# Regrouping the first loads on two hardware queues, whole score stages, and a remade instruction order, in a hashed-attention and feed-forward kernel

## The chip, the cores and the metric

The kernel runs on one core of one Trainium2 chip. The time is device microseconds of one execution; a run's time is 1.7 to 2.8 us (mostly 1.7) longer than the span of its profile, which runs from the first to the last instruction. Before the change the median of 3 runs was 319.82 us (319.4 to 319.95). Differences of a per cent are discussed here, so kernels that are compared ran on the same chip in the same rounds. All ratios are the mean time of one kernel's fast runs over the mean of the other's fast runs of the same rounds, so they are not quite the ratios of the medians quoted beside them.

## The reference

```python
# q, k, v: (4, 8, 768, 64) float32, proj: (64, 6), w_ch1: (512, 2048), w_ch2: (2048, 512)
q_bits = (q @ proj > 0);  k_bits = (k @ proj > 0)            # 6 hash bits for each row
mask   = bucket(q_bits)[..., :, None] == bucket(k_bits)[..., None, :]
scores = where(mask, q @ k.T / 8, -1e9)
attn   = softmax(scores)                                     # row sum + 1e-9
x      = (attn @ v)  -> (4, 768, 512)
xn     = (x - mean) / sqrt(var + 1e-6) * g_ln
out    = x + relu(xn @ w_ch1) @ w_ch2
```

(Shortened.) The attention of a batch feeds a feed-forward block on the same rows.

## The kernel before

The kernel is a list of words, each of which emits one small group of instructions. A word is `name.engine.arguments`; engines are `t` TensorE, `v` VectorE, `a` ScalarE, `p` GpSimd and `s` the queue of SyncE. Every engine executes its own words strictly in the order of the list; only tile dependences join the engines. The whole schedule is thus that list, and changing it is changing the program.

```python
def lx(eng, g, t, kp):              # one third of q (t=0) or k (t=1) of batch 0, head group g: 256 KB
    src = qk_view(t, 0, g).rearrange("p (c kp x) -> p kp c x", c=CC, kp=3)
    dst = Xt(0, g, t).rearrange("p (c kp x) -> p kp c x", c=CC, kp=3)
    eng.dma_start(out=dst[:, kp], in_=src[:, kp])
def lv(eng, b, hs, c):              # V of 4 heads, 32 partitions: 192 KB
    eng.dma_start(out=vnat(b, hs)[32*c:32*c+32], in_=v_view[b][c][:, hs:hs+4])
def tn(eng, g, t, kp): ...          # VectorE: 32x32 transposes of a third of batch 0      X  -> tp
def tu(eng, b, g, t, n): ...        # VectorE: the same for batches 1 to 3                  X  -> T
def ca(...), CA(...): ...           # cast to bf16, on VectorE, ScalarE or GpSimd           tp/T -> qb, kb
def ha(...); def bi(...)            # TensorE hash product hf; VectorE makes its bits G
def cv(...); def su(...)            # GpSimd: V to bf16 (vaug); three additions to vsum
def sp(...); def sc(...)            # TensorE vp <- vsum; copy to vsB (a correction of the row sums)
# ... cut ...
def S_(eng, s, h): ...              # scores of stage s; h=0, 1: two heads each, h=2: all four
def E_(eng, s, h): ...              # ScalarE: exponential of two heads
def A_(eng, s, h): ...              # attention times V, summed in PSUM over 6 stages of a unit
def na, nb, nc_, ce: ...            # VectorE: y; division x <- y,rc; statistics; xc <- x,mv,gB
def fl(eng, u, t): ...              # DMA transpose xnT <- xc (unit 0: TensorE "ft" and a copy "fc")
def F_(eng, u, p): ...              # first layer, f <- xnT,w_sb: 8 matmuls
def R_(eng, u, p): ...              # relu hb <- f, on VectorE or ScalarE
def D_(eng, u, t, qtr): ...         # second layer, f <- w_sb,hb: 4 matmuls
def Z_(...); def O_(...)            # res on VectorE; the output's DMA
```

The work is 12 units of 256 rows, each with 6 score stages. The first layer of unit 0 can start only when stages 0 to 5 have been multiplied with V, divided and normalised; from then on the matmuls of one unit fill the gaps of the next one's attention.

The softmax here doesn't subtract the row's maximum and nothing guards it: scores larger than these inputs give would overflow.

Of the kernel before, what the change touches and what calls it, by code (L numbers as in the profile page):

```python
# [17 lines left out]
mem.v lp.a pf.v lx.s.0.1.1 warm.t tn.v.0.1.1 lx.s.0.0.0 tn.v.0.0.0 ca.a.0.0.0 ha.t.0.0.0 lx.s.0.1.0 tn.v.0.1.0  # L18
pmem.p lx.s.1.0.0 lx.s.0.0.1 lx.s.0.1.2 bi.v.0.0.0 lx.s.1.1.1 lx.s.1.1.0 p32.p lv.s.0.0.0 lv.s.0.0.1 ha.t.0.1.0
bi.v.0.1.0 lv.s.0.0.2 lv.s.0.0.3 on.p.0 ha.t.0.1.1 ca.a.0.1.0 S.t.0.0 S.t.0.1 E.a.0.0 lx.s.1.1.2 bi.v.0.1.1 E.a.0.1  # L20
ca.p.0.1.1 tn.v.0.1.2 ha.t.0.1.2 tn.v.1.0.0 tn.v.1.1.0 S.t.1.0 ca.v.1.0.0 S.t.1.1 E.a.1.1 ca.v.0.1.2 tn.v.1.1.1
ha.t.1.1.0 E.a.1.0 lv.s.0.4.3 lx.s.1.0.1 bi.v.0.1.2 ha.t.1.1.1 bi.v.1.1.1 S.t.2.1 E.a.2.1 S.t.2.0 lv.s.0.4.0
ca.p.1.1.1 ca.v.1.1.0 ha.t.1.0.0 bi.v.1.0.0 cv.p.0.0.0 cv.p.0.0.2 A.t.1.1 A.t.2.1 A.t.0.1 su.p.0.0 A.t.0.0 E.a.2.0
A.t.2.0 S.t.4.0 E.a.4.0 S.t.4.1 E.a.4.1 lv.s.0.4.1 tn.v.1.0.1 tn.v.0.0.1 ha.t.0.0.1 A.t.1.0 tn.v.1.1.2 ca.p.1.1.2
lg.s lx.s.1.0.2 ca.v.0.0.1 bi.v.1.1.0 sp.t.0.0 sc.v.0.0 S.t.3.0 ha.t.1.1.2 E.a.3.0 na.v.0.0 nb.v.0.0 S.t.3.1 E.a.3.1
bi.v.1.1.2 S.t.5.0 ha.t.1.0.1 E.a.5.0 S.t.5.1 bi.v.0.0.1 S.t.6.0 ca.v.1.0.1 tn.v.1.0.2 ca.v.1.0.2 lw1.p.2 lx.s.0.0.2
tn.v.0.0.2 ca.v.0.0.2 lv.s.0.4.2 cv.p.0.4.2 A.t.4.1 cv.p.0.4.0 A.t.4.0 A.t.3.0 A.t.5.0 nc.v.0.0 bi.v.1.0.1 A.t.3.1
on.p.1 E.a.5.1 S.t.7.1 A.t.5.1 su.p.0.4 sp.t.0.4 sc.v.0.4 na.v.0.1 nb.v.0.1 lw1.p.1 lw1.p.0 E.a.6.0 S.t.8.0 E.a.7.1
S.t.6.1 A.t.6.0 lw1.p.3 E.a.8.0 S.t.9.0 A.t.8.0 lv.s.1.4.1 lw2.p.2 E.a.6.1 A.t.6.1 E.a.9.0 S.t.8.1 E.a.8.1 S.t.7.0
E.a.7.0 S.t.9.1 E.a.9.1 A.t.7.1 A.t.8.1 lw2.p.1 lw2.p.0 A.t.7.0 lv.s.1.4.0 LX.s.1.0.0 tu.v.1.0.0.3 tu.v.1.0.0.0  # L30
tu.v.1.0.0.1 tu.v.1.0.0.2 nc.v.0.1 ce.v.0.1 ft.t.0.1 fc.a.0.1 ce.v.0.0 rs.p.0 ft.t.0.0 S.t.11.2 E.a.11.1 E.a.11.0
lw2.p.3 LX.s.1.0.1 tu.v.1.0.1.0 tu.v.1.0.1.1 tu.v.1.0.1.3 lv.s.1.4.2 fc.v.0.0 F.t.0.5 F.t.0.4 R.v.0.5 F.t.0.3
R.v.0.4 R.a.0.3 S.t.10.2 E.a.10.0 F.t.0.2 R.a.0.2 tu.v.1.0.1.2 CA.p.1.0.1 na.v.1.0 A.t.9.0 A.t.11.2 nb.v.1.0
nc.v.1.0 A.t.9.1 ha.t.0.0.2 bi.v.0.0.2 E.a.10.1 A.t.10.2 na.v.1.1 nb.v.1.1 nc.v.1.1 ce.v.1.0 fl.s.1.0 ce.v.1.1
fl.s.1.1 F.t.0.0 R.a.0.0 F.t.0.1 R.a.0.1 S.t.14.2 E.a.14.0 E.a.14.1 hm.t.1.0 bt.v.1.0 mo.s.1.0.0.2 mo.s.1.0.1.2
mo.s.1.0.2.1 mo.s.1.0.0.3 F.t.0.7 R.a.0.7 F.t.0.6 R.a.0.6 A.t.14.2 S.t.13.2 E.a.13.0 LX.s.1.1.0 mo.s.1.0.3.2
D.t.0.0.0 D.t.0.0.1 D.t.0.0.2 E.a.13.1 A.t.13.2 S.t.12.2 E.a.12.1 F.t.1.0 R.a.1.0 mo.s.1.0.1.3 D.t.0.0.3 Z.v.0.0
F.t.1.7 mo.s.1.0.3.3 CA.p.1.0.0 tu.v.1.1.0.0 tu.v.1.1.0.3 ha.t.1.0.2 bi.v.1.0.2 LX.s.1.1.1 tu.v.1.1.1.0 tu.v.1.1.1.2
tu.v.1.1.1.3 lv.s.1.0.1 rs.p.1 lv.s.1.4.3 su.p.1.4 E.a.12.0 tu.v.1.1.0.1 mo.s.1.0.0.1 mo.s.1.0.1.0 mo.s.1.0.2.3
mo.s.1.0.1.1 mo.s.1.0.3.1 R.a.1.7 F.t.1.5 R.a.1.5 S.t.16.2 E.a.16.0 tu.v.1.1.1.1 mo.s.1.0.2.2 A.t.12.2 E.a.16.1  # L40
lv.s.1.0.2 mo.s.1.0.2.0 mo.s.1.0.3.0 lv.s.1.0.3 F.t.1.4 R.a.1.4 lv.s.1.0.0 cv.p.1.0.2 cv.p.1.4.0 D.t.0.1.0 S.t.17.2
E.a.17.0 E.a.17.1 mo.s.1.0.0.0 tu.v.1.1.0.2 CA.v.1.1.0 hm.t.1.1 bt.v.1.1 mo.s.1.1.2.1 mo.s.1.1.3.3 mo.s.1.1.0.0
mo.s.1.1.0.2 mo.s.1.1.1.1 D.t.0.1.1 mo.s.1.1.3.0 cv.p.1.0.0 sp.t.1.4 sc.a.1.4 mo.s.1.1.2.3 S.t.15.2 E.a.15.0
E.a.15.1 na.v.2.0 A.t.17.2 A.t.16.2 nb.v.2.0 nc.v.2.0 mo.s.1.1.1.3 F.t.1.1 D.t.0.1.2 mo.s.1.1.3.1 tab.a R.v.1.1
mo.s.1.1.3.2 A.t.15.2 na.v.2.1 nb.v.2.1 nc.v.2.1 ce.v.2.1 ce.v.2.0 rs.p.2 fl.s.2.1 fl.s.2.0 F.t.1.2 R.a.1.2
mo.s.1.1.0.1 S.t.18.2 E.a.18.0 E.a.18.1 CA.v.1.1.1 D.t.0.1.3 Z.v.0.1 mo.s.1.1.1.2 F.t.1.3 R.a.1.3 mo.s.1.1.1.0
S.t.20.2 E.a.20.1 E.a.20.0 F.t.1.6 A.t.18.2 su.p.1.0 D.t.1.0.0 D.t.1.0.1 D.t.1.0.2 R.v.1.6 sp.t.1.0 sc.a.1.0
S.t.19.2 E.a.19.1 E.a.19.0 F.t.2.0 R.v.2.0 D.t.1.0.3 Z.v.1.0 mo.s.1.1.2.2 mo.s.1.1.0.3 F.t.2.2 R.v.2.2 on.p.2
mo.s.1.1.2.0 S.t.22.2 E.a.22.0 E.a.22.1 A.t.20.2 F.t.2.7 R.v.2.7 D.t.1.1.0 S.t.21.2 E.a.21.0 E.a.21.1 LX.s.2.0.0
tu.v.2.0.0.0 D.t.1.1.1 LX.s.2.0.1 tu.v.2.0.1.0 tu.v.2.0.1.2 LX.s.2.1.0 F.t.2.4 O.s.0.2 R.a.2.4 tu.v.2.0.0.3 O.s.0.0  # L50
A.t.19.2 na.v.3.0 nb.v.3.0 LX.s.2.1.1 S.t.23.2 E.a.23.1 F.t.2.1 R.v.2.1 O.s.0.3 nc.v.3.0 cv.p.1.4.2 lv.s.2.4.0
lv.s.2.4.2 lv.s.2.0.3 lv.s.2.0.1 lv.s.2.0.2 lv.s.2.4.3 A.t.22.2 lv.s.2.4.1 A.t.21.2 tu.v.2.0.1.3 F.t.2.3 R.v.2.3
E.a.23.0 A.t.23.2 na.v.3.1 nb.v.3.1 nc.v.3.1 ce.v.3.0 fl.s.3.0 S.t.25.2 E.a.25.0 E.a.25.1 F.t.2.5 R.a.2.5
tu.v.2.0.1.1 D.t.1.1.2 D.t.1.1.3 S.t.24.2 E.a.24.0 E.a.24.1 F.t.2.6 R.a.2.6 A.t.25.2 Z.v.1.1 O.s.1.0 D.t.2.0.0
O.s.1.2 O.s.1.3 ce.v.3.1 fl.s.3.1 CA.v.2.0.1 tu.v.2.0.0.1 S.t.26.2 E.a.26.0 E.a.26.1 D.t.2.0.1 O.s.0.1 tu.v.2.0.0.2
LX.s.3.0.1 hm.t.2.0 bt.v.2.0 mo.s.2.0.1.0 mo.s.2.0.0.3 mo.s.2.0.2.1 mo.s.2.0.3.1 mo.s.2.0.0.0 mo.s.2.0.1.2
mo.s.2.0.2.0 mo.s.2.0.0.1 mo.s.2.0.3.2 S.t.28.2 E.a.28.0 E.a.28.1 F.t.3.2 R.v.3.2 su.p.2.4 A.t.26.2 A.t.24.2
na.v.4.0 nb.v.4.0 F.t.3.4 R.v.3.4 CA.p.2.0.0 tu.v.2.1.1.3 tu.v.2.1.0.0 tu.v.2.1.0.1 S.t.27.2 E.a.27.1 E.a.27.0
tu.v.2.1.0.3 mo.s.2.0.0.2 LX.s.3.1.1 D.t.2.0.2 D.t.2.0.3 Z.v.2.0 F.t.3.3 R.a.3.3 tu.v.2.1.1.2 A.t.27.2 S.t.29.2
E.a.29.1 cv.p.2.4.0 nc.v.4.0 F.t.3.0 R.v.3.0 A.t.28.2 D.t.2.1.0 mo.s.2.0.1.1 F.t.3.1 R.v.3.1 lv.s.2.0.0 cv.p.2.0.0  # L60
cv.p.2.0.2 mo.s.2.0.1.3 O.s.1.1 mo.s.2.0.3.0 E.a.29.0 A.t.29.2 S.t.30.2 E.a.30.0 E.a.30.1 na.v.4.1 nb.v.4.1 F.t.3.7
R.a.3.7 D.t.2.1.1 D.t.2.1.2 S.t.32.2 E.a.32.1 mo.s.2.0.2.2 F.t.3.5 A.t.30.2 nc.v.4.1 ce.v.4.1 fl.s.4.1 ce.v.4.0
fl.s.4.0 R.v.3.5 D.t.2.1.3 Z.v.2.1 O.s.2.2 O.s.2.0 su.p.2.0 F.t.3.6 R.v.3.6 E.a.32.0 A.t.32.2 mo.s.2.0.3.3
tu.v.2.1.1.1 S.t.31.2 E.a.31.0 E.a.31.1 tu.v.2.1.0.2 CA.p.2.1.0 LX.s.3.0.0 F.t.4.5 R.v.4.5 D.t.3.0.0 mo.s.2.0.2.3
F.t.4.6 R.v.4.6 rs.p.4 S.t.33.2 E.a.33.0 O.s.2.3 O.s.2.1 D.t.3.0.1 tu.v.2.1.1.0 CA.p.2.1.1 LX.s.3.1.0 hm.t.2.1
bt.v.2.1 mo.s.2.1.2.3 mo.s.2.1.0.2 mo.s.2.1.2.0 mo.s.2.1.3.2 mo.s.2.1.2.1 tu.v.3.0.1.3 mo.s.2.1.3.1 mo.s.2.1.2.2
mo.s.2.1.3.0 mo.s.2.1.0.1 mo.s.2.1.1.3 mo.s.2.1.1.2 mo.s.2.1.0.0 E.a.33.1 S.t.34.2 E.a.34.0 E.a.34.1 F.t.4.0 R.v.4.0
tu.v.3.0.0.0 D.t.3.0.2 D.t.3.0.3 sp.t.2.0 sc.a.2.0 rs.p.3 A.t.31.2 na.v.5.0 Z.v.3.0 S.t.35.2 E.a.35.0 E.a.35.1
F.t.4.3 R.v.4.3 tu.v.3.0.1.0 A.t.33.2 mo.s.2.1.1.1 A.t.34.2 nb.v.5.0 nc.v.5.0 tu.v.3.0.0.3 F.t.4.2 R.a.4.2 A.t.35.2
na.v.5.1 on.p.3 S.t.37.2 E.a.37.0 E.a.37.1 F.t.4.7 R.a.4.7 mo.s.2.1.1.0 D.t.3.1.0 D.t.3.1.1 S.t.36.2 E.a.36.1  # L70
E.a.36.0 D.t.3.1.2 D.t.3.1.3 F.t.4.1 R.a.4.1 tu.v.3.0.1.2 nb.v.5.1 S.t.38.2 E.a.38.0 nc.v.5.1 ce.v.5.1 fl.s.5.1
ce.v.5.0 rs.p.5 fl.s.5.0 A.t.37.2 F.t.4.4 R.a.4.4 mo.s.2.1.0.3 mo.s.2.1.3.3 Z.v.3.1 O.s.3.0 O.s.3.3 O.s.3.1
D.t.4.0.0 D.t.4.0.1 tu.v.3.0.1.1 CA.p.3.0.1 F.t.5.3 R.v.5.3 A.t.36.2 E.a.38.1 S.t.39.2 E.a.39.1 E.a.39.0 F.t.5.4
R.v.5.4 D.t.4.0.2 D.t.4.0.3 Z.v.4.0 S.t.40.2 E.a.40.0 E.a.40.1 tu.v.3.0.0.2 F.t.5.0 R.v.5.0 A.t.38.2 na.v.6.0
nb.v.6.0 D.t.4.1.0 sp.t.2.4 sc.a.2.4 O.s.3.2 S.t.41.2 E.a.41.0 E.a.41.1 F.t.5.6 cv.p.2.4.2 A.t.40.2 lv.s.3.4.1
A.t.39.2 lv.s.3.4.2 lv.s.3.4.3 R.v.5.6 F.t.5.7 R.a.5.7 S.t.42.2 E.a.42.1 E.a.42.0 A.t.41.2 F.t.5.1 R.a.5.1
lv.s.3.0.1 D.t.4.1.1 D.t.4.1.2 lv.s.3.0.0 nc.v.6.0 S.t.44.2 E.a.44.0 F.t.5.2 R.a.5.2 D.t.4.1.3 na.v.6.1 A.t.42.2
# [41 lines left out]
def kernel(  # L119
# [15 lines left out]
    nc = tc.nc  # L135
# [13 lines left out]
    A = 4 * (D + 1)  # L149
# [139 lines left out]
    def lx(eng, g, t, kp):  # L289
        src = qk_view(t, 0, g).rearrange("p (c kp x) -> p kp c x", c=CC, kp=3)  # L290
        dst = Xt(0, g, t).rearrange("p (c kp x) -> p kp c x", c=CC, kp=3)
        eng.dma_start(out=dst[:, kp], in_=src[:, kp])  # L292
# [254 lines left out]
```

## Time and profile before

| | profile before | timed |
|---|---|---|
| span or time | 325.0 us (its own run took 326.67) | 319.82 us |
| mean granted clock | 0.957 | |
| first first-layer matmul | 51.65 us | |

The profile that was at hand before the prediction fell in an execution with a longer stretch of half clock. Its lines must not be compared with a fast profile directly; a fast profile of the same kernel was taken later (called "the control" below, span 318.9 us).

From the profile page of the kernel before: the slices (40 equal ones, busy tenths), the granted TensorE clock, the DMA share, and what was moved.

```profile
span 325.0 us, 9793 instructions
...
PE   6869999999989999999999999999999999999993
...
PEclk9995558999999999999999999999999999999999
DMA  7999799146117981463154140111220400402122
GB/s 198 216 219 275 130 205 162 23 133 165 51 38 272 302 189 57 144 173 119 22 146 86 32 117 0 39 25 23 53 53 2 114 20 2 99 2 48 50 67 65
```

TensorE looks full after the first five slices. The three 5s in the clock are the slow stretch (24 to 51 us). The DMA engines are busy from the second slice to the seventh, at 130 to 275 GB/s, 201 in the mean. The table of windows of the kernel before says of the later part (columns: the window, its length, busy us and instruction count of each engine, clock, DMA share, GB/s):

```profile
200.00:300.00 100.00, 100.00 (x1474) 67.68 (x1472) 54.71 (x105) 61.41 (x69) 14.44 (x17) 1.00 0.17 38
```

TensorE has no idle time there at full clock. Two groups of the kernel before that matter later (line, engine, operation, tiles, shapes, count; busy us and mean ns of one; idle time before and what ended it):

```profile
L487 DVE TENSOR_SCALAR hb<-f 128x512 bf16<-128x512 f32 x53 | 36.6, 691 | 63.8 <-PE f L477 63.5
...
L442 DVE TENSOR_TENSOR x<-y,rc 128x512 f32<-128x512 f32 x24 | 18.4, 767 | 0.8
```

Source line numbers shift by three or four from one version to another; the tile names are what identifies a line.

### The profile page before, as it was taken

The page shows a single profiled execution, that of the slowest core. Times are in us where ns is not written, and L with a number is a line of the kernel's source. Part 1 is how long each engine was busy: PE and PEld are TensorE (multiplying, and loading weights), DVE is VectorE, ACT ScalarE, POOL GpSimd, SP SyncE. Part 2 cuts the span into 40 slices and gives each one's busy share as a digit, 9 for nine tenths or more (in the row PEclk, how much of TensorE's full clock was granted, in tenths as well). Part 3 has the DMA queues.
Part 4 walks back from the last instruction along what each step waited for, and adds up shares of the span by engine and source line. Part 5 has one row for each costly group of instructions (what it writes and reads, how often), then busy time and mean ns, then how long its engine had stood idle before and what let it go on. Part 6 is the DMA issues. An engine that isn't in the chain of part 4 may idle for free.

```text
span 325.0 us, 9793 instructions
## 1 busy us (share of the span) xinstructions
PE 310.7 (96%) x4320; PEld 211.8 (65%) x4320; DVE 182.9 (56%) x356; ACT 182.0 (56%) x198; POOL 91.5 (28%) x102
## 2 busy tenths in 40 slices
PE   6869999999989999999999999999999999999993
PEld 6555767766656767657677667666667666766651
DVE  4547475716645958765825628914635546446441
ACT  3553476666456676646756656764776675771000
POOL 2065822603470054474220056700300100001000
PEclk9995558999999999999999999999999999999999
DMA  7999799146117981463154140111220400402122
GB/s 198 216 219 275 130 205 162 23 133 165 51 38 272 302 189 57 144 173 119 22 146 86 32 117 0 39 25 23 53 53 2 114 20 2 99 2 48 50 67 65
DMA packets 33354, 33.59 MB, mean 103 GB/s; under 512 B 15648, under 2 KB 29984, under 8 KB 33312
## 3 DMA queue, kind: packets, MB, share of 16 engines
q1 hardware_dynamic: 29008, 28.77, 34.9%
q0 software_dynamic: 4224, 4.19, 8.0%
q8 instruction: 34, 0.56, 0.8%
q14 instruction: 8, 0.07, 0.1%
q10 hardware_dynamic: 80, 0.00, 0.0%
HBM read 27.53 MB, written 6.29 MB: 104 GB/s over the span
## 4 chain that ended last, share of the span: by engine, by line
PE 78%; DMA 8%; DVE 6%; SPq 4%; POOL 2%; issue 1%; ACT 0%; DVEq 0%; ACTq 0%
PE f L477 24%; PE f L492 23%; PE sc L405 17%; PE acc L420 11%; DMA X<-in_q_dram 4%; DMA vn<-in_v_dram 3%; SPq L382 2%; PE hp L370 2%; DVE xc L450 2%; DMA X<-in_k_dram 2%; PE hf L306 2%; SPq L292 1%; DVE st L446 1%; DVE x L442 1%; DVE y L433 1%
## 5 line engine op out<-in xcount | busy, mean ns | idle before, releaser
L411 ACT ACTIVATE E<-sc,bias_sb 128x1024 bf16<-128x1024 f32 x144 | 153.7, 1111 | 82.2 <-PE sc L405 80.3
L477 PE MATMUL f<-xnT,w_sb 128*128 128x256 bf16 x768 | 99.2, 273 | 0.5 <-DVE hb L487 0.5
L492 PE MATMUL f<-w_sb,hb 128*128 128x512 bf16 x384 | 93.6, 379 | 0.0
L477 PEld LDWEIGHTS <-w_sb 128*128 128x128 bf16 x768 | 70.8, 98 | 23.4 <-issue 9.9
L487 DVE TENSOR_SCALAR hb<-f 128x512 bf16<-128x512 f32 x53 | 36.6, 691 | 63.8 <-PE f L477 63.5
L405 PE MATMUL sc<-qb,kb 32*128 32x256 bf16 x1152 | 62.9, 281 | 0.0
L492 PEld LDWEIGHTS <-hb 128*128 128x128 bf16 x384 | 35.6, 98 | 35.4 <-issue 3.8
L405 PE MATMUL sc<-G 6*128 6x256 bf16 x576 | 48.6, 285 | 0.4 <-ACT E L411 0.2
L420 PEld LDWEIGHTS <-E 128*128 128x128 bf16 x1152 | 43.3, 100 | 8.0 <-issue 5.1
L420 PE MATMUL acc<-vaug,E 128*128 128x65 bf16 x1152 | 46.9, 198 | 0.2 <-POOL vaug L328 0.2
L405 PEld LDWEIGHTS <-kb 32*128 32x128 bf16 x1152 | 35.5, 98 | 3.2
L485 ACT ACTIVATE hb<-f 128x512 bf16<-128x512 f32 x43 | 25.6, 596 | 20.6 <-PE f L477 20.5
L455 POOL TENSOR_SCALAR rs<-mv 128x2 f32<-128x2 f32 x12 | 8.5, 710 | 98.1 <-DVE mv L449 97.8
L497 DVE SCALAR_TENSOR_TENSOR res<-f,rs,x 128x512 f32<-128x512 f32 x24 | 17.9, 745 | 28.3 <-PE f L492 21.6
L405 PEld LDWEIGHTS <-G 6*128 6x128 bf16 x576 | 17.3, 94 | 22.4 <-issue 19.5
L244 DVE STREAM_TRANSPOSE T<-X 128x384 f32<-128x384 f32 x48 | 24.9, 553 | 3.6 <-DMA X<-in_k_dram 3.4
L336 POOL TENSOR_TENSOR t<-vn 128x768 f32<-128x768 f32 x8 | 15.2, 1905 | 34.6 <-DMA vn<-in_v_dram 20.2
L328 POOL CAST vaug<-vn 128x768 bf16<-128x768 f32 x16 | 13.9, 889 | 39.0 <-DMA vn<-in_v_dram 30.3
L433 DVE SCALAR_TENSOR_TENSOR y<-vsB,acc 128x520 f32<-128x520 f32 x24 | 16.5, 689 | 9.0 <-PE acc L420 8.7
L450 DVE SCALAR_TENSOR_TENSOR xc<-x,mv,gB 128x512 bf16<-128x512 f32 x24 | 19.9, 829 | 0.9
L306 PE MATMUL hf<-tp,pfull 128*128 128x256 f32 x48 | 15.1, 447 | 5.2 <-DVE tp L244 4.2
L442 DVE TENSOR_TENSOR x<-y,rc 128x512 f32<-128x512 f32 x24 | 18.4, 767 | 0.8
(49 smaller groups left out, 153.1 us busy)
## 6 DMA issues: line engine op xcount, KB each, us to landing
vn<-in_v_dram SPq DMA_DIRECT2D x32, 192.0 KB
out_dram<-res SPq DMA_DIRECT2D x44, 128.0 KB
X<-in_q_dram SPq DMA_DIRECT2D x6, 768.0 KB
X<-in_k_dram SPq DMA_DIRECT2D x6, 768.0 KB
w_sb<-in_moe_w_ch_dram POOLq DMA_DIRECT2D x8, 512.0 KB, 11.1
X<-in_k_dram SPq DMA_DIRECT2D x6, 256.0 KB
X<-in_q_dram SPq DMA_DIRECT2D x6, 256.0 KB
G<-B SPq DMA_DIRECT2D x96, 4.5 KB
```

What stands on the lines that cost most here:

```text
L244: nc.vector.transpose(d[:, j], s[:, j, kj0 : kj0 + n])
L306: nc.tensor.matmul(hf(g, t, kp)[:, :256], pfull[:, j], tp(g, t, kp)[:, j], start=(j == 0), stop=(j == 1))
L405: nc.tensor.matmul(sc(s, i // 2)[:, i % 2, 256 * kk : 256 * kk + 256], lh, rh, start=(rep == 0), stop=(rep == 2), skip_group_check=True,)
L411: nc.scalar.activation(E(s)[:, heads(h)], sc(s, h), AF.Exp, scale=EXP_SCALE, bias=bias_sb)
L420: nc.tensor.matmul(acc[:, qt, (D + 1) * i : (D + 1) * (i + 1)], E(s)[:, i, 256 * kk + P * qt : 256 * kk + P * qt + P], vaug(u // 3)[:, 4 * ...
L433: nc.vector.scalar_tensor_tensor(yt(u, g), vs, EPS_ROW, made[f"acc{u}{g}"][:, :, :A], op0=AOP.mult, op1=AOP.add,)
L442: nc.vector.tensor_tensor(xo, a[:, :, :, 0:D], rc.to_broadcast([P, 2, 4, D]), op=AOP.mult)
L450: nc.vector.scalar_tensor_tensor(xc(u)[:, t], xt(u)[:, t], mv(u)[:, t, 0:1], gB, op0=AOP.subtract, op1=AOP.mult,)
L477: nc.tensor.matmul(f1[:, n].rearrange("p (t x) -> p t x", t=2), w1_sb[:, dt, P * nt : P * nt + P], xnT(u)[:, :, dt], start=(dt == 0), stop ...
L485: nc.scalar.activation(hb(u)[:, 2 * p : 2 * p + 2], f1, AF.Relu)
L487: eng.tensor_scalar_max(hb(u)[:, 2 * p : 2 * p + 2], f1, 0.0)
L492: nc.tensor.matmul(f2, hb(u)[:, nt, P * t : P * t + P], w2_sb[:, nt], start=(nt == 0), stop=(nt == NNT - 1),)
```

## The change

The intent: bring the data of batch 0 in fewer, larger transfers over both hardware queues; emit the scores, and the products with V, of the first ten stages for four heads at once; and let the first layer start after 9 score stages instead of 11. The whole list of words was made anew for this. The code changes little:

```diff
-    def lx(eng, g, t, kp):
-        src = qk_view(t, 0, g).rearrange("p (c kp x) -> p kp c x", c=CC, kp=3)
-        dst = Xt(0, g, t).rearrange("p (c kp x) -> p kp c x", c=CC, kp=3)
-        eng.dma_start(out=dst[:, kp], in_=src[:, kp])
+    def lx(eng, g, t, kp0, kp1):
+        src = qk_view(t, 0, g).rearrange("p (c kp x) -> p c kp x", c=CC, kp=3)
+        dst = Xt(0, g, t).rearrange("p (c kp x) -> p c kp x", c=CC, kp=3)
+        eng.dma_start(out=dst[:, :, kp0:kp1], in_=src[:, :, kp0:kp1])
```

The head of the list (the list has 1,113 words, before 1,138; those that follow are in another order too; cut):

```diff
-mem.v lp.a pf.v lx.s.0.1.1 warm.t tn.v.0.1.1 lx.s.0.0.0 tn.v.0.0.0 ca.a.0.0.0 ha.t.0.0.0 lx.s.0.1.0 tn.v.0.1.0
-pmem.p lx.s.1.0.0 lx.s.0.0.1 lx.s.0.1.2 bi.v.0.0.0 lx.s.1.1.1 lx.s.1.1.0 p32.p lv.s.0.0.0 lv.s.0.0.1 ha.t.0.1.0
-bi.v.0.1.0 lv.s.0.0.2 lv.s.0.0.3 on.p.0 ha.t.0.1.1 ca.a.0.1.0 S.t.0.0 S.t.0.1 E.a.0.0 lx.s.1.1.2 bi.v.0.1.1 E.a.0.1
 ... cut ...
+lx.s.0.1.0.1 on.p.0 mem.v lx.s.0.0.0.1 pmem.p tn.v.0.1.0 warm.t lx.s.0.1.1.3 lx.s.1.0.0.1 lp.a pf.v lv.s.0.4.3
+ca.a.0.1.0 lv.a.0.0.0 lv.s.0.0.3 lv.a.0.4.1 tn.v.0.0.0 ca.a.0.0.0 ha.t.0.1.0 bi.v.0.1.0 lv.a.0.0.1 ha.t.0.0.0
+bi.v.0.0.0 S.t.0.2 E.a.0.1 E.a.0.0 lv.s.0.0.2 tn.v.0.1.1 ha.t.0.1.1 ca.p.0.1.1 tn.v.0.1.2 ca.p.0.1.2 ha.t.0.1.2
+lx.a.0.0.1.3 tn.v.1.0.0 ca.v.1.0.0 cv.p.0.0.2 p32.p bi.v.0.1.1 S.t.1.2 E.a.1.0 bi.v.0.1.2 ha.t.1.0.0 bi.v.1.0.0
+cv.p.0.0.0 A.t.0.2 lw1.p.2 E.a.1.1 S.t.2.2 E.a.2.1 E.a.2.0 lx.s.1.1.0.3 tn.v.1.1.2 ca.p.1.1.2 tn.v.1.1.1 tn.v.1.1.0
+ca.v.1.1.1 ca.v.1.1.0 ha.t.1.1.1 bi.v.1.1.1 ha.t.1.1.0 LX.s.1.0.1 tu.v.1.0.1.0 tu.v.1.0.1.1 tu.v.1.0.1.3
 ... cut ...
```

At the end of the list five output transfers go to ScalarE's queue.

## The prediction

> What bounds it now. By the table of windows, TensorE is busy 199.5 of the 200 us between 100 and 300 at full clock: nothing can be won there. Costing every group at its full-clock step in the chain of waits (relu-layer group of 8 matmuls 0.87 us, second-layer group of 4 0.86, four-head score 0.77, attention-times-V 0.49, hash group about 0.95), all TensorE work comes to about 287 us, 67 of it before 100 us. So some 33 us are lost in the first 100 us of the profiled run (span 325.0). That run had the clock at 0.50 from 24.1 to about 51 us (timeline slices and windows); the timed runs (319.8) are some 7 us shorter, so I take them as mostly unthrottled, with about 26 us lost, nearly all before the first layer of unit 0 starts (51.7 us in the profile, by my estimate 44 to 45 in a timed run). There the limits are: DMA engines saturated from 2 to 32 us at only 180 to 300 GB/s; ScalarE, which needs 2 x 1.11 us of exponentials for each score stage; and TensorE's own order (it waits from 20.8 to 23.2 us for a q transpose that the next scores do not need). The Trainium skill, "TensorE: Matmul & The Clock Gate" (HAM clock gate), says that idle windows halve the clock; the trace agrees: 0.50 just after that gap.
>
> What changes. (1) Scores and products of ten stages go from two halves to whole: two halves took 1.08 us against 0.77, so about 3 us of TensorE, but in a stretch where TensorE is not the limit. (2) Batch-0 q/k loads: 12 issues of 256 KB (0.55 to 0.72 us of queue each) become 7; six loads move to ScalarE's queue. The skill's "DMA: Bandwidth & Descriptors" (Issuing engines are not separate DMA queues) says that both queues share the same 16 engines; the trace, saturated with one queue alone, agrees, so I expect only 1 to 2 us from issue time and longer runs, not a doubled rate. (3) The order: first layer after 9 score stages instead of 11; the q kp1 hash comes after the scores of unit 0; weights are requested from about 14 us on instead of 25 and 35; all V of batch 1 is requested early; V loads still come as 32-partition pieces at about 200 GB/s. The counts of matmuls, exponentials and elementwise work stay.
>
> Estimate. First layer of unit 0 starts at 36 to 37 us, held by the 768 KB k load (about 17 us), then by the batch-1 k load, for whose transposes VectorE waits before the bits of stage 3 (about 24 us), then by 2.2 us of ScalarE per stage. TensorE has then done about 22 us of work; 265 remain, plus 4 to 5 us of switches and a wait for the third weight chunk, plus about 4.8 us of tail and 1.7 us between span and time: about 313. Output issues split over two queues at the end save perhaps 0.5 us.
>
> Prediction: 313 us, 8 in 10 between 306.5 and 318.5. Chances: over 2% faster 0.52, within 2% 0.45, slower 0.03.
>
> Signs. Windows: TensorE saturated from about 40 us on; work after 100 us unchanged at about one lost us in 200. First first-layer matmul at 33 to 40 us. ScalarE exponentials of the first six stages done by about 30 us. DMA share near full until 45 to 50 us, same GB/s for V.
>
> What would make it wrong: a clock at 0.50 in the timed runs of one kernel only (up to 8 us either way); early batch-1 and weight loads delaying the last k load or the first weights (the gain vanishes); or loads much faster than 250 GB/s with longer runs (first layer near 31 us, time near 307).

## The result

| | before, same job | after |
|---|---|---|
| median | 319.88 us (319.4 to 320.76, 4 runs) | 329.13 us (328.3 to 330.21, 4 runs) |
| ratio | | 1.0288, 95% interval 1.0247 to 1.0329 |
| profile | (slow one, above) | span 327.0 us, clock 0.976 |

The kernel became slower by 2.9%, against a predicted gain of 2%; the time lies well outside the range. A second measurement of the same file gave 1.0239 (below). From the profile page of the kernel after, the same lines:

```profile
span 327.0 us, 9752 instructions
...
PE   6737879989979989999999999799999999899994
...
PEclk9769799999999999999999999999999999999998
DMA  6999999311289737120129014121210210402222
GB/s 173 172 272 241 213 304 280 59 36 28 85 149 288 191 87 260 25 51 8 38 65 289 17 38 94 33 55 25 60 42 2 51 49 2 98 2 43 56 64 64
```

The mean clock is not the reason: it is 0.976 here and 0.977 in the control. In the first 50 us both have stretches at half clock (by windows of 1 us about 11 to 14, 18 to 24 and 35 to 38 us here, 7 to 10 and 35 to 45 in the control); after 60 us both run at full clock, but for the last microseconds. TensorE's line has digits of 8 and less in all of its first six slices and, sparsely, much later. A caution: the trace has 342 records of the second layer's 384 matmuls, so the busy share of TensorE itself proves nothing; recorded waits are used instead.

The groups of the kernel after that answer to those of before, with two of TensorE:

```profile
L474 PE MATMUL f<-xnT,w_sb 128*128 128x256 bf16 x768 | 99.5, 273 | 6.9 <-DMA xnT<-xc 3.4
...
L484 DVE TENSOR_SCALAR hb<-f 128x512 bf16<-128x512 f32 x62 | 42.7, 689 | 72.7 <-PE f L474 72.4
...
L417 PE MATMUL acc<-vaug,E 128*128 128x65 bf16 x1152 | 45.8, 196 | 5.2 <-POOL vaug L325 5.2
...
L439 DVE TENSOR_TENSOR x<-y,rc 128x512 f32<-128x512 f32 x24 | 23.8, 991 | 0.8
```

Nine relus moved to VectorE (62 against 53). The divisions, of the same shape and count, take 991 ns in the mean against 767. The first layer waits 6.9 us where it waited 0.5 before.

**Where the time went, as two terms.** Cut each profile at the first first-layer matmul. The line of it in the control, in the kernel after, and in an experiment that has the new order to about 60 us and the old one after that (h_newstart):

```profile
45.13 2.10 PE L474 MATMUL f<-xnT,w_sb 128*128 128x256 bf16 x17
```
```profile
46.38 1.80 PE L474 MATMUL f<-xnT,w_sb 128*128 128x256 bf16 x15
```
```profile
44.47 1.80 PE L473 MATMUL f<-xnT,w_sb 128*128 128x256 bf16 x15
```

The prediction of 313 us is a span of 311.3 (less 1.7), and put this matmul at 36.5; so it left 274.8 us for the rest. Measured: 46.4 and 327.0 - 46.4 = 280.6. The error is 9.9 us in the start and 5.8 us in the rest, 15.7 together. How it splits depends on the profile: a second one of the same file (a_control, below) gives 7.8 and 8.0. The control has 45.1 and 318.9 - 45.1 = 273.8; h_newstart has 44.5 and 318.6 - 44.5 = 274.1. So the start was not made slower by much: it failed to become faster. The loss against the kernel before lies in the rest.

**The start of the kernel after.** From its timeline (start, length, engine, line, operation, count; in brackets the idle time before it and what ended it), one fence for each of ScalarE, TensorE, VectorE and GpSimd:

```profile
16.31 0.62 ACTq L289 DMA_DIRECT2D X<-in_q_dram  x1
16.98 2.12 ACT L408 ACTIVATE E<-sc,bias_sb 128x1024 bf16<-128x1024 f32 x2 [5.63 <-DMA vn<-in_v_dram]
...
35.08 2.12 ACT L408 ACTIVATE E<-sc,bias_sb 128x1024 bf16<-128x1024 f32 x2 [2.14 <-PE sc L402]
```
```profile
14.57 0.39 PE L402 MATMUL sc<-qb,kb 32*128 32x256 bf16 x8
...
21.26 1.04 PE L417 MATMUL acc<-vaug,E 128*128 128x65 bf16 x16 [5.25 <-POOL vaug L325]
```
```profile
22.32 4.16 DVE L252 CAST kb<-tp 128x512 bf16<-128x512 f32 x2
...
30.79 2.17 DVE L439 TENSOR_TENSOR x<-y,rc 128x512 f32<-128x512 f32 x1
...
41.09 0.69 DVE L439 TENSOR_TENSOR x<-y,rc 128x512 f32<-128x512 f32 x1
```
```profile
23.50 1.82 POOL L333 TENSOR_TENSOR t<-vn 128x768 f32<-128x768 f32 x1
...
30.61 1.79 POOL L333 TENSOR_TENSOR t<-vn 128x768 f32<-128x768 f32 x1
```

Three things are to be seen. First, stage 1's scores are done at 14.96, but its exponential starts at 16.98: a q load stands before it in ScalarE's stream, and its issue came only at 16.31, when a V load had landed. (In the program as built, each hardware load waits for the completion of an earlier one whose semaphore it reuses, eight issues back, counted over both queues; that is read from the program, the trace shows the wait.) Secondly, TensorE stands 5.25 us before the product of stage 0 for V, with the scores of stage 2 behind it. Thirdly, VectorE's two casts take 4.16 us (a scaled cast of the same size takes 0.43 at 38.73) and its division 2.17 us instead of 0.69, each time beside GpSimd's additions of V. The Trainium skill, "SBUF — State Buffer", section "Who interferes with whom", says that VectorE and GpSimd share one pair of SBUF ports under an exclusive lock, and that a VectorE instruction with two SBUF inputs contends with a GpSimd instruction that reads SBUF. This trace agrees: the division that starts at 30.79 ends 0.56 us after GpSimd's addition of 30.61 has ended, and 0.69 is all it needs alone.

On the two queues the prediction was right. Windows of the control and then of the kernel after (as above; DMA share and GB/s are the last two columns):

```profile
20.00:40.00 20.00, 17.36 (x252) 12.18 (x251) 16.38 (x39) 12.81 (x12) 13.73 (x19) 0.87 1.10 236
```
```profile
20.00:40.00 20.00, 15.12 (x235) 11.21 (x234) 16.47 (x29) 8.84 (x9) 16.98 (x20) 0.79 1.09 229
```

236 GB/s with one queue, 229 with two, the DMA engines saturated in both (201 and 198 in the 20 us before that). The Trainium skill, "DMA: Bandwidth & Descriptors", section "Issuing engines are not separate DMA queues", says that transfers of all issuing engines interleave on the same 16 DMA engines, and this agrees.

**The rest.** The table of waits of TensorE after 60 us (tile waited for, total us, times, longest), for the kernel after and for h_newstart, which does the same work there in the old order:

```profile
PE f L474 <- DMA xnT<-xc: 3.4, 3, 1.6
PE f L474 <- DVE hb L484: 1.9, 2, 1.6
PE f L474 <- ACT E L408: 1.2, 1, 1.2
PE f L489 <- issue: 0.6, 4, 0.2
PE f L489 <- DVE res L494: 0.5, 1, 0.5
...
```
```profile
PE f L488 <- issue: 1.1, 7, 0.2
PE f L473 <- DMA xnT<-xc: 0.7, 1, 0.7
PE f L473 <- DVE hb L483: 0.3, 1, 0.3
...
```

All rows sum to 8.8 us in the first and 2.5 in the second. The difference, 6.3 us, is near the difference of the two rests (280.6 - 274.1 = 6.5). So close an agreement is partly luck: a_control, the same file as the kernel after, has waits of 9.4 us, 6.9 more than h_newstart, and a rest that is 8.7 longer; n_start2 (below) has waits of 5.0 and a rest of 276.3. Most of what the new order loses after 60 us is thus TensorE standing for the transposed, normalised rows (xnT) and for relus and residuals of VectorE (6.6 of the 8.8). Of the 8.8 us, 5.9 lie after 100 us, where the control has 0.4. One such place, in the timeline of the kernel after (GpSimd, VectorE twice, the DMA queue of SyncE, TensorE):

```profile
58.80 4.12 POOL L250 TENSOR_SCALAR qb<-T 128x1536 bf16<-128x1536 f32 x1 [1.95 <-DVE T L241]
```
```profile
60.31 2.28 DVE L439 TENSOR_TENSOR x<-y,rc 128x512 f32<-128x512 f32 x1
...
64.56 0.78 DVE L447 SCALAR_TENSOR_TENSOR xc<-x,mv,gB 128x512 bf16<-128x512 f32 x1
```
```profile
64.44 2.62 SPq L456 DMA_TRANSPOSE xnT<-xc  x2
```
```profile
68.41 1.03 PE L474 MATMUL f<-xnT,w_sb 128*128 128x256 bf16 x8 [0.93 <-DMA xnT<-xc]
```

The second half of xc is ready at 65.34, the first layer of that unit starts at 68.41, and TensorE waited 0.93 us of these 3.1. The division before it was stretched by 1.6 us beside GpSimd's cast of 4.12 us.

### The profile page after: what moved, and what is told of

Read it like the earlier page. It is cut to its first block, busy times and chain, and to the rows that moved or that the text cites. A ratio compares the mean times of both kernels' runs of the same rounds, so it can differ in the third digit from the quotient of the medians.

```text
span 327.0 us, 9752 instructions
## 1 busy us (share of the span) xinstructions
PE 295.8 (90%) x4278; PEld 205.3 (63%) x4320; DVE 195.5 (60%) x363; ACT 176.1 (54%) x189; POOL 94.2 (29%) x104
## 4 chain that ended last, share of the span: by engine, by line
PE 62%; DVE 19%; DMA 10%; SPq 3%; issue 3%; ACT 1%; POOL 0%; DVEq 0%; POOLq 0%; ACTq 0%
PE f L474 22%; PE f L489 18%; PE sc L402 11%; PE acc L417 8%; DMA vn<-in_v_dram 4%; DVE x L439 3%; DVE xc L447 3%; DVE hb L484 2%; DVE T L241 2%; DMA xnT<-xc 2%; DMA X<-in_q_dram 2%; PE hp L367 2%; DVE st L443 2%; SPq L379 1%; DMA out_dram<-res 1%
## 5 line engine op out<-in xcount | busy, mean ns | idle before, releaser
L489 PE MATMUL f<-w_sb,hb 128*128 128x512 bf16 x342 | 86.1, 379 | 3.4 <-issue 0.6
L484 DVE TENSOR_SCALAR hb<-f 128x512 bf16<-128x512 f32 x62 | 42.7, 689 | 72.7 <-PE f L474 72.4
L402 PE MATMUL sc<-qb,kb 32*128 32x256 bf16 x1152 | 52.9, 270 | 0.0
L402 PE MATMUL sc<-G 6*128 6x256 bf16 x576 | 41.6, 276 | 5.2 <-DVE G L244 3.7
L452 POOL TENSOR_SCALAR rs<-mv 128x2 f32<-128x2 f32 x12 | 6.3, 524 | 101.9 <-DVE mv L446 101.6
L402 PEld LDWEIGHTS <-kb 32*128 32x128 bf16 x1152 | 30.4, 94 | 1.8
L402 PEld LDWEIGHTS <-G 6*128 6x128 bf16 x576 | 15.3, 92 | 24.7 <-issue 17.1
L482 ACT ACTIVATE hb<-f 128x512 bf16<-128x512 f32 x34 | 20.3, 596 | 15.0 <-PE f L474 14.7
L250 POOL TENSOR_SCALAR qb<-T 128x1536 bf16<-128x1536 f32 x5 | 20.5, 4105 | 18.1 <-DVE T L241 18.1
L439 DVE TENSOR_TENSOR x<-y,rc 128x512 f32<-128x512 f32 x24 | 23.8, 991 | 0.8
L447 DVE SCALAR_TENSOR_TENSOR xc<-x,mv,gB 128x512 bf16<-128x512 f32 x24 | 21.5, 897 | 0.8
```

What stands on the lines that cost most here:

```text
L250: eng.tensor_scalar(dst, src, QS, None, op0=AOP.mult)
L402: nc.tensor.matmul(sc(s, i // 2)[:, i % 2, 256 * kk : 256 * kk + 256], lh, rh, start=(rep == 0), stop=(rep == 2), skip_group_check=True,)
L439: nc.vector.tensor_tensor(xo, a[:, :, :, 0:D], rc.to_broadcast([P, 2, 4, D]), op=AOP.mult)
L447: nc.vector.scalar_tensor_tensor(xc(u)[:, t], xt(u)[:, t], mv(u)[:, t, 0:1], gB, op0=AOP.subtract, op1=AOP.mult,)
L482: nc.scalar.activation(hb(u)[:, 2 * p : 2 * p + 2], f1, AF.Relu)
L484: eng.tensor_scalar_max(hb(u)[:, 2 * p : 2 * p + 2], f1, 0.0)
```

## The experiments

Eighteen kernels ran in five jobs; those of one job share a chip and the runs of the kernel before. All results were correct (the two that leave out the sums of V still stayed within the tolerance). "F0" is the start of the first first-layer matmul; "rest" is the span less F0.

| label | median us | ratio to before | 95% interval | F0 | rest |
|---|---|---|---|---|---|
| b_control | 321.82 | 1.0019 | 0.9935 to 1.0102 | 45.1 | 273.8 |
| b_group | 319.2 | 0.9939 | 0.9838 to 1.0040 | 45.2 | 273.1 |
| a_oldloads | 335.59 | 1.0357 | 1.0243 to 1.0472 | 53.2 | 283.5 |
| a_s2first | 329.3 | 1.0251 | 1.0175 to 1.0327 | 45.3 | 283.0 |
| h_newstart | 321.61 | 0.9987 | 0.9931 to 1.0043 | 44.5 | 274.1 |
| h_newrest | 341.63 | 1.0542 | 1.0457 to 1.0628 | 46.8 | 294.0 |
| a_nosu | 324.97 | 1.0078 | 1.0008 to 1.0148 | 44.1 | 279.7 |
| b_nosu | 319.62 | 0.9906 | 0.9845 to 0.9966 | 41.5 | 272.8 |
| a_start | 339.53 | 1.0547 | 1.0494 to 1.0601 | 57.3 | 281.3 |
| a_rest | 326.5 | 1.0124 | 1.0055 to 1.0193 | 47.2 | 278.5 |
| a_both | 339.04 | 1.0526 | 1.0470 to 1.0583 | 55.2 | 280.8 |
| n_start | 335.99 | 1.0414 | 1.0335 to 1.0494 | 57.1 | 278.4 |
| a_control | 328.74 | 1.0239 | 1.0188 to 1.0291 | 44.3 | 282.8 |
| a_start2 | 329.42 | 1.0241 | 1.0173 to 1.0309 | 47.7 | 282.0 |
| a_both2 | 328.74 | 1.0117 | 1.0041 to 1.0194 | 43.3 | 279.1 |
| n_start2 | 320.7 | 1.0000 | 0.9931 to 1.0070 | 42.9 | 276.3 |
| n_start3 | 321.82 | 1.0045 | 1.0012 to 1.0078 | 44.6 | 276.1 |
| a_both3 | 325.79 | 1.0174 | 1.0144 to 1.0204 | 43.0 | 282.3 |

(Two of the four runs of a_both2 were slow, so its median is not that of its ratio. Two of the four runs of a_oldloads were slow as well, its profile among them. All the profiles hold some half-clock time before 60 us, most of all a_oldloads, a_start, n_start and the others with a clock near 0.96, so F0 and rest of one profile are good to 2 to 5 us only. The same file gave 46.4 (after) and 44.3 (a_control), and kernels whose words are the same up to F0 differ as much: a_start2, a_both2 and n_start2 have 47.7, 43.3 and 42.9. No difference of F0 under that size is read as an effect here.)

### First job: loads or order?

**b_control**: the kernel before, unchanged.

> The kernel before itself, unchanged, for a profile that may fall in the unthrottled state and as the noise of the comparison. All theories: ratio 1.00 within 0.5%. If a trace comes at clock 1.0 between 24 and 51 us, the first layer of unit 0 should start at 44 to 45 us and span be about 318.

It measured 1.0019, and its fast profile has the first first-layer matmul at 45.13 us. The prediction's estimate of 44 to 45 us for a timed run of the kernel before is met, but partly by luck: the condition of the expectation was not. This profile too is at half clock from about 35 to 45 us, so 45.1 is not an undisturbed start.

**b_group**: the old order with the new, larger transfers, all on one queue.

```diff
-lx.s.0.1.1 ... lx.s.0.0.0 ... lx.s.0.1.0 ... (12 loads of 256 KB)
+lx.s.0.1.0.1 ... lx.s.0.0.0.1 ... lx.s.0.1.1.3 ... (7 loads of 256 to 768 KB)
-tn.v.0.1.1 ... tn.v.0.1.0
+tn.v.0.1.0 ... tn.v.0.1.1
```

> Before's compute order, all loads still on SP's queue, only the 12 q/k loads of batch 0 regrouped to 7 as in the change. Theory L (the larger transfers themselves cost: the k load of the second head group lands whole and late): slower by 3 us or more. Theory O (the remade order costs, not the transfers): within 1.5 us of before.

It measured 0.9939 with 1 inside the interval: regrouping alone does no harm, and what good it may do is under what this job can tell.

**a_oldloads**: the new order with the loads of before (sizes, sequence, one queue).

> The changed kernel's compute order, but batch-0 loads in before's sizes, sequence and queue (12 q/k pieces, all on SP). Theory L: most of the 9 us comes back, time near 321. Theory O: stays at 326 to 330.

It measured 1.0357 and F0 at 53.2 us. The new order with the old loads is if anything worse than with the new ones. Together with b_group, and with h_newstart below, which has the new loads on both queues and is as fast as the kernel before: the loads are not what made the kernel slower; the order is.

**a_s2first**: the most conspicuous wait taken away.

```diff
-A.t.0.2 lw1.p.2 E.a.1.1 S.t.2.2 E.a.2.1 E.a.2.0
+lw1.p.2 E.a.1.1 S.t.2.2 E.a.2.1 E.a.2.0 A.t.0.2
```

> The changed kernel with one word moved: the scores of stage 2 go ahead of the product of stage 0 on TensorE, so TensorE no longer waits 5.2 us for V before them. Theory A (this wait is the loss of the start): exponentials of stage 2 at about 19 us instead of 23.8, and 3 to 5 us off the time. Theory D (the next limit, the late k load and VectorE's casts stretched while GpSimd works, ends last anyway): under 1.5 us off.

It measured 1.0251, which is the kernel after (1.0239 and 1.0288). TensorE no longer waits 5.2 us for V before stage 2, and nothing comes of it: F0 is at 45.3. The longest single wait of the start was not what set its length.

### Second job: start or rest, and the sums of V

**h_newstart**: the new order up to the first hash product of batch 1 (about 60 us), the old order for all that was left.

> The changed order up to the first hash group of batch 1 (about 60 us), then before's order for all the rest. It splits the loss by place. Theory S (the loss is made in the start): 327 or more, as the changed kernel. Theory P (it is made on both sides, by VectorE held up while GpSimd reads SBUF, and by first-layer groups placed too close behind their transposes): start costs 2 to 4 us, so 322 to 325. If it is all in the rest: 320.

It measured 0.9987. The start of the change, with its two queues, its whole score stages and its three visible waits, costs what the old start costs. Since it differs from the kernel after only behind 60 us, the loss lies there: 1.0239 and 1.0288 against 0.9987, some 7 to 9 us (328.74 against 321.61 us on one chip). The fourth job repeats this with another start, within one job: a_start2 and n_start2 differ in the rest alone and measured 1.0241 and 1.0000.

**h_newrest**: the reverse, the old order up to that point and the new one behind it.

> Before's order up to the same point (about 60 us), then the changed order for the rest. Theory S: 320 to 321. Theory P: the rest costs 4 to 6 us, so 324 to 327.

It measured 1.0542, but it is not a fair test: the new rest counts on batch-1 loads that the old start has not requested, and TensorE waits 8.9 and 5.3 us at the seam. Its result is left out of the argument.

**a_nosu and b_nosu**: the three GpSimd additions of each half of V (about 3.4 us, eight times) replaced by a memset to zero, in the kernel after and in the one before. The result lacks a correction of the row sums.

```diff
-        nc.gpsimd.tensor_tensor(t3, s[:, 0:3], s[:, 3:6], op=AOP.add)
-        nc.gpsimd.tensor_tensor(t3[:, 0], t3[:, 0], t3[:, 1], op=AOP.add)
-        nc.gpsimd.tensor_tensor(vsum(b)[...], t3[:, 0], t3[:, 2], op=AOP.add)
+        nc.gpsimd.memset(vsum(b)[:, D * hs : D * (hs + 4)], 0.0)
```

> The changed kernel with GpSimd's sums of V (three tensor_tensor, 3.4 us, eight times) replaced by one memset each: the uniform-row correction is then zero on purpose, which shows in no row that has a match. In the trace of the changed kernel, VectorE's two-input and cast instructions took 13.8 us longer than their usual time, each time under such a GpSimd instruction or a GpSimd cast; 5.4 us in before. Theory P: the stretches under the sums go and the time falls by 3 to 6 us, far more than in b_nosu. Theory Q (stretches are off the critical path): falls by under 1.5 us, or as much as b_nosu.

> Before with the same sums of V replaced by memsets. All theories: its critical path meets few stretches, so it gains 0 to 2 us; the difference of the two gains is what the sums cost the new order more than the old one.

The kernel after goes from 1.0239 or 1.0288 to 1.0078, the one before from 1.0019 to 0.9906. So the additions cost the new order some 1.6 to 2.1% and the old one 1.1%, which would account for 1.5 to 3 us of the 7 to 9 that were lost; each ratio is good to 0.4 to 0.8%, so this share is not clear of zero. In a_nosu the two casts of VectorE that took 4.16 us take 1.41, and the waits for relus (hb) fall to 0.9 us; but those for xnT rise from 3.4 (4.5 in a_control) to 5.3 us, so the rest is only a little shorter. The additions cost time in both kernels. How much of it goes by the port lock is not separated from a rival: with the additions go TensorE's waits for their sums (1.4 us after 60 us in the control). Either way they are the smaller part of the difference between the kernels: without the sums in both, the new order is still 1.7% slower (1.0078 against 0.9906, same job). A count in h_newstart agrees:

```profile
L438 DVE TENSOR_TENSOR x<-y,rc 128x512 f32<-128x512 f32 x24 | 23.2, 965 | 0.8
```

Its divisions are stretched as much as those of the kernel after (965 against 991 ns), since most of the stretching lies before 60 us (5.0 of 6.6 us over the usual 0.69 each), and yet it is as fast as the kernel before.

### Third job: repairs by hand

**a_start** makes four repairs in the start: scores of stage 2 first; two casts to ScalarE; all loads on one queue; the bits of stage 3 ahead of the batch-1 transposes. **a_rest** repairs what TensorE waited for after 60 us: five first-layer groups come a little later, the normalisation of unit 2 comes ahead of an output it stood behind, and some GpSimd work moves. **a_both** has both; **n_start** is h_newstart with the start repairs.

```diff
 a_start
-A.t.0.2 ... S.t.2.2 E.a.2.1 E.a.2.0
+S.t.2.2 E.a.2.1 E.a.2.0 A.t.0.2
-ca.v.1.1.1 ca.v.1.1.0
+ca.a.1.1.1 ca.a.1.1.0
-lv.a.... lx.a....
+lv.s.... lx.s....          (in place)
 a_rest
-F.t.1.4 R.v.1.4 A.t.14.2 ha.t.1.0.2 bi.v.1.0.2
+A.t.14.2 ha.t.1.0.2 bi.v.1.0.2 F.t.1.4 R.v.1.4
-Z.v.0.1 ... nb.v.2.1 nc.v.2.1 ce.v.2.0 ce.v.2.1 fl.s.2.0 fl.s.2.1
+nb.v.2.1 nc.v.2.1 ce.v.2.0 ce.v.2.1 fl.s.2.0 fl.s.2.1 ... Z.v.0.1
 ... cut ...
```

> The changed kernel with four repairs of its start and nothing else: scores of stage 2 ahead of the product of stage 0; the two k casts of the last k load on ScalarE instead of VectorE (where they were held 4.2 us under GpSimd); the six loads of ScalarE's queue back on SP, so that no exponential waits behind a load's issue; the bits of stage 3 ahead of the batch-1 transposes. Theory R (the start can be won, and each of these was a real loss): first layer at 38 to 42 us instead of 46.4, and 4 to 7 us off the time, near 323. Theory T (something else holds the start, such as V or the weights): first layer still after 44 us and under 2 us off.

> The changed kernel with repairs only after 60 us: four first-layer groups that TensorE waited at for their transposed input (0.9, 1.6, 1.2, 0.8 us) moved one or two groups later, unit 2's normalisation ahead of an output that waits for TensorE, and three pieces of GpSimd work moved away from VectorE's two-input instructions. Theory P (the rest lost some 7 us by these waits): TensorE's recorded waits after 60 us fall from 7.5 to under 3 us and 4 to 6 us come off, near 324. Rival (other waits take their place): under 2 us off.

> Both sets of repairs together. If the two losses are independent, the gains add: 9 to 12 us off, 317 to 320, back at before or a little under it. If the loss of one hides that of the other, no better than the better of the two.

> The hybrid of the changed start and before's rest (0.9987 of before), with the four repairs of the start. If they are worth what they are in the changed kernel: 4 to 7 us under before, near 315, ratio 0.98; this is then what the prediction had expected of the change.

Three of the four are a miss of mine. Moved "in place" to the one queue, a late q load came to stand behind batch-1 V loads, which wait for a buffer that batch 0 still holds; TensorE then waited 12.1 us for its transposes, and F0 went to 57 us. That says nothing on the theories, and the ratios of a_start, a_both and n_start (1.0547, 1.0526, 1.0414) are those of this mistake. a_rest alone is a result: 1.0124, about half of the loss recovered. I had expected TensorE's waits after 60 us to fall under 3 us; they fell from 8.8 to 6.5. Those for xnT were gone, and waits for relus (2.8 and 1.3 us) and for residuals (0.9 and 0.7) stood in their place.

### Fourth job: the repairs without the mistake

**a_control** is the kernel after once more. **start2** means: batch-0 loads all on one queue and ahead of batch 1's, the large k load of the second head group ahead of V, two casts on ScalarE, the first product with V behind the scores of stage 4, the bits of stage 3 earlier. a_start2 is the kernel after with it, a_both2 adds a_rest's repairs, n_start2 is h_newstart with it.

```diff
-lx.a.0.0.1.3, lx.a.1.0.1.3, lx.s.1.1.0.3 and lv.*.0.*  spread over two queues
+lp.a lx.s.1.1.0.3 lv.s.0.0.0 ... lv.s.0.0.3 lx.s.0.0.1.3 lv.s.0.4.0 ... lv.s.0.4.3 lx.s.1.0.1.3
-ca.v.1.1.1 ca.v.1.1.0
+ca.a.1.1.1 ca.a.1.1.0
-A.t.0.2 ... S.t.4.2
+S.t.4.2 A.t.0.2
-bi.v.1.1.0 sp.t.0.0
+ha.t.1.1.0 bi.v.1.1.0
```

> The changed kernel itself, unchanged, beside the others on one chip, because the kernel before moved from 319.9 to 321.7 us between chips. All theories: ratio 1.02 to 1.03, with first layer at 45 to 47 us.

> The start repaired again, with the mistake of the first try undone (there q loads stood on SP behind loads that wait for a free buffer): all batch-0 loads on SP, the last k load ahead of all V, q's second parts ahead of the batch-1 loads; k casts on ScalarE; product of stage 0 after the scores of stage 4; bits of stage 3 ahead of the batch-1 transposes. Theory R (late k load, held casts and waits in order made the start): first layer at 38 to 42 us, 4 to 7 us under a_control. Theory T (V or the weights limit): first layer at 44 us or later, within 2 us of a_control.

> a_start2 with the repairs after 60 us of a_rest. Theory P (the rest's waits are worth 3 to 5 us by themselves): 3 to 5 us under a_start2. If a_rest's gain was drift between chips: under 1.5 us.

> Before's rest behind this repaired start. If Theory R holds: 4 to 7 us under before, ratio 0.98. Theory T: within 1 us of before.

The kernel after gave 1.0239 again. With the start's repairs it gave 1.0241, with those of the rest too 1.0117, and with the old rest 1.0000. F0 of a_start2 is no earlier, 47.7. Stages 0 to 2 and 4 now have their exponentials at 9, 12, 15 and 19 us in n_start2; but F0 is still 42.9. The table of VectorE's waits (n_start2, up to 50 us) and that of TensorE's (up to 60 us) say where the time went:

```profile
DVE T L240 <- DMA X<-in_k_dram: 7.1, 1, 7.1
```
```profile
PE vp L339 <- POOL vsum L334: 3.3, 1, 3.3
PE hf L302 <- DVE vsB L349: 2.4, 1, 2.4
```

VectorE stands until 24.7 us for the batch-1 k load, with the correction vsB and the bits of stages 3 and 5 behind it, and TensorE stands for GpSimd's sums and then for VectorE.

### Fifth job: those waits taken away too

**n_start3** and **a_both3** move the batch-1 transposes behind the first division of unit 0, and the scores of stages 3 and 5 ahead of the product with the sums.

```diff
-LX.s.1.0.1 tu.v.1.0.1.0 tu.v.1.0.1.1 tu.v.1.0.1.3 tu.v.1.0.1.2 ... sp.t.0.0 sc.v.0.0 na.v.0.0 nb.v.0.0 nc.v.0.0
-S.t.3.2 E.a.3.0 E.a.3.1 ha.t.1.1.2 bi.v.1.1.2 S.t.5.2
+ha.t.1.1.2 bi.v.1.1.2 S.t.4.2 ... S.t.3.2 ... S.t.5.2 ... E.a.3.0 E.a.3.1 ... sp.t.0.0 sc.v.0.0 na.v.0.0 nb.v.0.0
+nc.v.0.0 tu.v.1.0.1.0 tu.v.1.0.1.1 tu.v.1.0.1.3 tu.v.1.0.1.2
```

> n_start2 (new start with single-queue loads, early k load, casts on ScalarE; old order from 60 us) with one thing more: VectorE's batch-1 k transposes, for whose load it waited 7.1 us, stand behind the first division of unit 0, and scores of stages 3 and 5 stand ahead of the product with GpSimd's sum of V. Theory T (the new start is held by VectorE and TensorE standing in program order behind late arrivals): the 7.1 us wait goes, the first first-layer matmul comes at 37 to 40 us (n_start2 42.9), the ratio to the kernel before is 0.98 to 0.99. Rival U (behind them the same time is taken by the next limit, the sums on GpSimd, V's loads or ScalarE's 2.2 us per stage): first layer at 41 us or later, ratio 0.995 or more. In both, recorded TensorE waits after 60 us stay near 2.3 us.

> The same start with the new order's rest and its repairs of a_rest. Theory T: first layer at 37 to 40 us (a_both2 43.3), ratio 1.0117 less about 0.01, so 0.998 to 1.005; the rest stays 4 to 7 us longer than n_start3's. Rival U: first layer at 41 us or later, ratio 1.01.

n_start3 measured 1.0045 and a_both3 1.0174: the rival. The 7.1 us wait is gone; the exponentials of the first six stages are over at 30.8 us, which is what the prediction had asked for. From the timeline of n_start3, ScalarE's sixth stage and TensorE's first first-layer matmul:

```profile
28.71 2.12 ACT L407 ACTIVATE E<-sc,bias_sb 128x1024 bf16<-128x1024 f32 x2 [1.61 <-PE sc L401]
```
```profile
44.55 0.83 PE L473 MATMUL f<-xnT,w_sb 128*128 128x256 bf16 x3
```

Yet 13.7 us pass from the end of these exponentials to the first layer. In the kernel after it was 9.2 (37.2 to 46.4). The time that the early stages gained was given back behind them, where the products of unit 0, its two divisions and its statistics on VectorE, and the hash and score work of stages 6 to 8 alternate between TensorE, VectorE and ScalarE in small steps.

A rival that no run separates: the clock. The granted clock of the control, of n_start2 and of n_start3, in slices of 8 us:

```profile
PEclk9899669999999999999999999999999999999999
```
```profile
PEclk9995899999999999999999999999999999999999
```
```profile
PEclk9997859999999999999999999999999999999999
```

Each start meets half clock at another place: the control at 35 to 45 us, n_start2 at 25 to 34, n_start3 at 27 to 30 and 37 to 47. Between the last of the first six exponentials and F0 the mean clock was 0.74 in n_start3 and 0.76 in a_both3, where this tail took 13.7 and 13.0 us; it was 0.93 or more in the kernel after, a_rest, a_nosu, a_both2 and n_start2, where the tail took 8.9 to 9.2. As an estimate (length times missing clock), up to 3.6 and 3.1 us of the two long tails are half clock, and some 10 us of each are not.

a_both3 against n_start3, with one start and two rests, gives the cost of the new rest once more, repaired as it is: 325.79 against 321.82, 4.0 us.

No version beat the kernel before beyond doubt: b_group at 0.9939 has 1 in its interval, and b_nosu at 0.9906 leaves out a part of the computation.

## Why the prediction was wrong, point by point

- **"First layer of unit 0 starts at 36 to 37 us"**: the first of two steps that failed. It came at 46.4 (44.3 in a_control, 44.5 in h_newstart), 9.9 us of the 15.7 by which the span was missed (7.8 of 15.8 in a_control). The step took three late arrivals one after the other, the k load, the batch-1 k load and ScalarE's 2.2 us a stage, and added about 6.5 us from the last exponential (by about 30 us) to the first layer. In the kernel after the last exponential ended at 37.2, 7.2 us later than asked, and the tail took 9.2 instead of 6.5, 2.7 more: together the 9.9. (These parts are of one profile, and no finer than the spread of F0 noted under the table of experiments.) The first term was held up by program order: a load in ScalarE's stream, V ahead of scores, VectorE's casts under GpSimd. These waits are shown. But taking them away one set after another (a_s2first, start2, n_start3) brought the exponentials to 30.8 us and F0 only to between 42.9 and 47.7. So the tail is mis-sized as well: it is not 6.5 us but about 9 at nearly full clock, and it was 13 and more where the exponentials came early. How much of those 13 is half clock, and how much is the small steps, is open.
- **"Work after 100 us unchanged at about one lost us in 200"**: the second step that failed, and the one that made a loss where otherwise only the gain would have been missing. The rest took 280.6 us against 274.8 predicted; after 100 us alone TensorE's recorded waits are 5.9 us against 0.4 in the control. I had read that nothing could be won where TensorE is saturated, and did not ask what a new order could lose there. h_newstart shows the loss directly, and the waits of TensorE after 60 us (8.8 or 9.4 against 2.5 us) have most of its size. a_rest recovers about half by moving words.
- **Two queues give no rate**: right (229 GB/s against 236 between 20 and 40 us). b_group and a_oldloads show that the regrouped loads do no harm and the order does.
- **Whole stages save about 3 us of TensorE where it is not the limit**: not tested by itself; h_newstart has them and equals the kernel before, which fits "not the limit".
- **The clock**: the timed runs of both kernels are comparable (0.974 to 0.99 in the four of the kernel after, 0.97 to 0.99 in the fast ones of the kernel before), so it does not explain the loss. But the prediction took the timed runs as "mostly unthrottled", and the control, whose timed run took 320.73 us, lost some 7 us of clock before F0 (45.13 us at 0.85), and the kernel after as much (46.38 at 0.85). The estimate of 36 to 37 us has no term for this.
- **The counts stay**: right, but nine relus went to VectorE, which I did not cost: its busy time rose from 182.9 to 195.5 us, of which the relus are 6.1 (42.7 - 36.6), the divisions 5.4 (23.8 - 18.4) and xc 1.6 (21.5 - 19.9).
- **"Slower: 0.03"** was too sure. The unknown that the prediction named, early loads in each other's way, was not the one that mattered.

What stays open: which of the small steps between the last exponential and the first layer sets the floor near 43 us, and whether any order of this start goes below it. My hand-made orders are three points, not a proof of a floor, and half clock is part of each of them. b_nosu came at 41.5 us with the old start, which may be GpSimd's sums or the clock: it was 0.93 before F0, against 0.85 in the control, and in the new order a_nosu came at 44.1, hardly earlier than a_control (44.3). Of the rest, 1.5 to 3 us go with the sums; for the remainder the waits are shown, but a cause common to them is not.

## What to carry to other kernels

A schedule that was tuned as a whole has a part that is already full; in that part a new order has next to nothing to win and can lose, so ask of every moved instruction what stands behind it, not only what it gains. A wait that is long in the profile is worth what remains when it is gone: here four of them in the start, of 2 to 7.1 us, were taken away one after another, and the first layer came at 42.9 to 47.7 us where it had come at 44.3 to 46.4. To find which part of a remade order costs, splice the two orders at a point where the work done is the same: it told more than any repair did.

## What the Trainium skill lacked or had wrong

- "DMA: Bandwidth & Descriptors", section "Issuing engines are not separate DMA queues": it agrees on the rate, but says of a second issuing engine only that it saves sequencer time. It lacks the cost: a load in a compute engine's stream can stand for an earlier load and hold the compute behind it. ScalarE idled 5.63 us before the exponential at 16.98, of which 2.0 were after its scores were ready, behind an issue at 16.31.
- "SBUF — State Buffer", section "Who interferes with whom": it agrees with the trace. Of sizes it has two ratios, 6.8 for VectorE and 1.5 for GpSimd; here a division of 0.69 us took 2.17 beside an addition of GpSimd (a ratio of 3.1) and two casts of 0.43 took 4.16 (4.8).
- "TensorE: Matmul & The Clock Gate", section "Part 1: The HAM clock gate (the "warmup" mystery)", says that a busy window restores the full clock. In the slow profile of the kernel before, the clock was 0.51 in the mean from 24 to 51 us although TensorE was recorded busy 26.73 of these 27 us, with score matmuls of 32 rows and hash matmuls in float32; it returned only when the first layer's full-array matmuls began at 51.65. That is no rule: in the kernel after the clock came back at about 14, 24 and 38 us, before any first-layer matmul. What counts as busy for such matmuls, the section does not say.
- No page that I read gives the time that a DMA transpose between SBUF tiles holds its queue, or that passes until its result can be used, for this chip: the issue took 1.19 to 2.42 us of the queue for 128 x 512 bf16, and in the place shown the first layer started 3.1 us after the second tile was ready to be transposed.
